# Pairing a gate chunk with a value chunk in one TensorE pass, with a new division of PSUM, in an attention and gated-MLP kernel

## The chip, the cores and the metric

The kernel runs on one core of one Trainium2 chip. The metric is the device time of one execution in microseconds (us), as the median of several executions. "PE" is TensorE (matmuls), "PEld" its weight loads, "DVE" VectorE, "ACT" ScalarE, "POOL" GpSimd.

## The reference, cut to what matters

```python
# x: (4, 12416, 128)   inducing: (32, 128)   4 x 12416 = 49664 tokens
def mab(q, kv):                       # softmax attention, no projections
    s = scale * (q @ kv.transpose(0, 2, 1))
    a = np.exp(s - s.max(-1, keepdims=True))
    a /= a.sum(-1, keepdims=True) + 1e-09
    return a @ kv
h = mab(inducing, x)                  # 32 rows for each batch
y = mab(x, h)                         # 12416 rows for each batch
# ... y as (49664, 128); d_ff = 1536
g   = y @ w_gate
val = y @ w_val
ffn = (gelu(g) * val) @ w_out
out = y + sigmoid(y @ w_res) * ffn
```

Each row of y is a mix of only 32 rows of h. So the kernel never forms y before the first layer: it multiplies h by the first-layer weights once for each batch, and the first layer of a token is then a matmul of its 32 attention weights (kept in four repeated row blocks of 32) with that small matrix.

## The kernel before

Tokens are taken in groups of 512: 24 for each of the four batches, numbered 0 to 23, and a small one of 128 tokens (24). A large group has six slots of two gate and two value chunks. The kernel divides eight PSUM banks of 128 x 512 f32: three buffers of two banks that gates and values share, and two single "side" banks.

```python
    ps_gv = ctx.enter_context(tc.tile_pool(name="psgv", bufs=3, space=bass.MemoryType.PSUM))
    ps_2 = [ctx.enter_context(tc.tile_pool(name=f"ps{i}", bufs=1, space=bass.MemoryType.PSUM))
            for i in range(2)]
    # ... cut
    def slot_mms(gi, si, weights):
        # ... cut: c0, cn, tw, half, rt
        v = wide_bank()
        for c in [i // 2 + (i % 2) * half for i in range(2 * half)]:
            if c < cn:
                r = slice(64, 128) if c >= half else slice(0, 64)
                pe.matmul(v[:, c * tw:(c + 1) * tw],
                          weights[b][r, (c0 + c) * P:(c0 + c + 1) * P], rt[r, :],
                          start=True, stop=True)
        return v[:, :cn * tw]

    def gate_slot(gi, si):
        v = slot_mms(gi, si, hg_t)
        # ... cut
        act.activation(ge[:, :n], v, AC.Gelu, bias=0.0, scale=1.0)        # 1024 wide

    def value_slot(gi, si):
        v = slot_mms(gi, si, hv_t)
        # ... cut
        ve.tensor_tensor(u[:, :n], ge_t.pop((gi, si)), v, AL.mult)        # 1024 wide
```

Two matmuls that use different halves of the array's 128 rows run at the same time (in the trace of this kernel, shown in the prediction, two of 512 columns take 0.39 us together, the line at 781.35). Before, two gate chunks share a pass, then two value chunks. At the end of a group two "mixes" of h (one for the sigmoid's argument, one for y) are made, each of four 128-column matmuls into a side bank, two slots and one slot before the group's last work (arguments shortened with ...):

```python
        def gate(self):
            bank = self.mix(hr_t[self.b])
            self.th = p_fin.tile([P, TOK], FP32, name="th", tag="th")     # p_fin: 2 buffers
            act.activation(self.th[:, :self.tw], bank[:, :self.tw], AC.Tanh, bias=0.0, scale=0.5)

        def residual(self):
            bank = self.mix(ha_t[self.b])
            self.at = p_fin.tile([P, TOK], FP32, name="at", tag="at")     # p_fin: 2 buffers
            act.activation(self.at[:, :self.tw], bank[:, :self.tw], AC.Copy, bias=0.0, scale=1.0)

        def end(self):
            ve.scalar_tensor_tensor(self.th..., self.ffn..., AL.add, AL.mult)     # (tanh + 1) * ffn
            po.tensor_tensor(self.at..., self.at..., self.th..., AL.add)
            sy.dma_start(out[...], self.at...)
    # ... cut: where each piece stands in the order of slots (f: the group's first slot)
            for i in range(6):
                at(f + 2 + i, lambda lg=lg: lg.mms(8))    # output matmuls
            at(f + 5, lg.gate, START)
            at(f + 6, lg.residual, START)
            at(f + 7, lg.end, LATE)
```

While one batch is worked on, the next one is prepared in the background: its scores and exponentials in two "bursts" (with slots that have values only, fed by gates stored ahead), five partial sums in between, and the sums of the second softmax (four reductions on VectorE).

The softmax here doesn't subtract the row's maximum and nothing guards it: scores larger than these inputs give would overflow.

Of the kernel before, what the change touches and what calls it, by code (L numbers as in the profile page):

```python
# [18 lines left out]
def kernel(  # L19
# [51 lines left out]
    p_ge = ctx.enter_context(tc.tile_pool(name="gelu", bufs=6))  # L71
    p_u = ctx.enter_context(tc.tile_pool(name="up", bufs=7))
    p_fin = ctx.enter_context(tc.tile_pool(name="fin", bufs=2))
    ps_gv = ctx.enter_context(tc.tile_pool(name="psgv", bufs=3, space=bass.MemoryType.PSUM))
    ps_2 = [ctx.enter_context(tc.tile_pool(name=f"ps{i}", bufs=1, space=bass.MemoryType.PSUM))
            for i in range(2)]

    ctx.enter_context(tc.manual_schedule())



    parity = [0]

    def side_bank(group):
        return ps_2[group % 2].tile([P, TOK], FP32, name="sb", tag="sb")

    def misc_bank():
        return side_bank(parity[0] + 1)

    def wide_bank():  # L90
        return ps_gv.tile([P, 2 * TOK], FP32, name="gv", tag="gv")
# [40 lines left out]
    def turn_pe(b, k):  # L132
        _, w = blocks_of(k)
        xt = sized(p_xt, w, P, "xt")
        xt_t[b, k] = xt
        tps = wide_bank().bitcast(FP16).rearrange("p (k c) -> p k c", c=P)
        for j in range(w):
            pe.transpose(tps[:, j, :], hi_t[b, k][:, j, :], identF)  # L138
        act.activation(xt[:, :w, :], tps[:, :w, :], AC.Copy, bias=0.0, scale=1.0)  # L139


    nacc_t, acc_t, ha_t, hr_t, hg_t, hv_t, ht_t, hf_t = {}, {}, {}, {}, {}, {}, {}, {}
    e_of = {}

    def scores(b, j0, j1, rows, bank):
        for j in range(j0, j1):
            k, jj = divmod(j, PRE)
            pe.matmul(bank[:, (j - j0) * M:(j - j0 + 1) * M], xt_t[b, k][:, jj, :], rows,  # L148
                      start=True, stop=True)

    def exp_a(b, j0, j1, bank=None):
        n = (j1 - j0) * M
        bank = wide_bank() if bank is None else bank
        scores(b, j0, j1, I1T, bank)
        if n > 2 * M:
            e1 = p_sm.tile([P, 2 * TOK], FP16, name="e1", tag="e1", bufs=3)
        else:
            e1 = p_sm.tile([P, 2 * M], FP16, name="e1s", tag="e1s", bufs=1)
        act.activation(e1[:, :n], bank[:, :n], AC.Exp, bias=0.0, scale=scale)
        for j in range(j0, j1):  # L160
            e_of["a", b, j] = e1[:, (j - j0) * M:(j - j0 + 1) * M]

    def accumulate(b, j0, j1, first, last):
        if first:
            acc_t[b] = misc_bank()
        acc = acc_t[b]
        for j in range(j0, j1):
# [3 lines left out]
            e = e_of.pop(("a", b, j))  # L171
            pe.matmul(o[:, 0:P], e, hi_t[b, k][:, jj, :],  # L172
                      start=(first and j < j0 + Q), stop=False, skip_group_check=True)
            pe.matmul(o[:, P:2 * P + 1], e, lo_t[b, k][:, jj, :P + 1],  # L174
                      start=False, stop=(last and j + Q >= j1), skip_group_check=True)
        if last:
            if b not in nacc_t:
                nacc_t[b] = p_h.tile([P, 2 * P + 1], FP32, name="nacc", tag="nacc", bufs=1)
                ve.tensor_copy(nacc_t[b], acc[:, :2 * P + 1])
            else:  # L180
                na = nacc_t[b]
                ve.tensor_tensor(na, acc[:, :2 * P + 1], na, AL.add)
            del acc_t[b]

    def finish_h(b):
        hs = misc_bank()
        na = nacc_t.pop(b)
        sm = strips.rearrange("p q m -> p (q m)")
        pe.matmul(hs[:, P:P + 1], sm, na[:, 2 * P:2 * P + 1], start=True, stop=True)
        pe.matmul(hs[:, 0:P], sm, na[:, 0:P], start=True, stop=False)  # L190
        pe.matmul(hs[:, 0:P], sm, na[:, P:2 * P], start=False, stop=True)
# [5 lines left out]
        ha = p_h.tile([P, P], FP16, name="ha", tag="ha")  # L197
        ha_t[b] = ha
        po.tensor_copy(ha, hf)
        po.tensor_tensor(ha[M:2 * M, :], hf[M:2 * M, :], ha[M:2 * M, :], AL.subtract)  # L200
        hg_t[b] = p_h.tile([P, F], BF16, name="hg", tag="hg")
        hv_t[b] = p_h.tile([P, F], BF16, name="hv", tag="hv")

    def turn_h(b):
        tp = misc_bank()
# [5 lines left out]
    def first_layer(b, parts, engs):  # L211

        bank = wide_bank()
        o = 0
        for (dst, w, c0, c1), eng in zip(parts, engs):
            o0 = o
            for c in range(c0, c1, TOK):
                e = min(c + TOK, c1)
                pe.matmul(bank[:, o:o + e - c], ht_t[b], w[:, c:e], start=True, stop=True)
                o += e - c  # L220
            if eng is act:
                act.activation(dst[:, c0:c1], bank[:, o0:o], AC.Copy, bias=0.0, scale=0.5)
            else:
                ve.tensor_scalar(dst[:, c0:c1], bank[:, o0:o], 0.5, None, op0=AL.mult)

    hgt_t = {}

    def first_layer_t(b):

        bank = wide_bank()  # L230
        for o, w in ((0, wG), (TOK, wV)):
            for c in range(FCH):
                pe.matmul(bank[:, o + c * M:o + (c + 1) * M], w[:, c * P:(c + 1) * P],
                          ht_t[b][:, 0:M], start=True, stop=True)
        hgt_t[b] = p_h.tile([P, 2, FCH * M], BF16, name="hgt", tag="hgt", bufs=1)
        act.activation(hgt_t[b], bank.rearrange("p (s n) -> p s n", s=2)[:, :, :FCH * M],
                       AC.Copy, bias=0.0, scale=0.5)

    def spread(b, i):

        n = 2 * FCH // 3
        src = hgt_t[b].rearrange("p s (c m) -> p (s c) m", m=M)[:, i * n:(i + 1) * n, :]
        a2 = p_sm.tile([P, PRE, Q, M], BF16, name="a2", tag="a2")
        po.tensor_copy(a2, src.unsqueeze(2).to_broadcast([P, n, Q, M]))
        for dst, c0, c1 in ((hg_t[b], 0, FCH), (hv_t[b], FCH, 2 * FCH)):
            lo, hi = max(c0, i * n), min(c1, (i + 1) * n)
            if lo < hi:
                sy.dma_start_transpose(
                    dst.rearrange("p (c f) -> p c f", f=P)[:, lo - c0:hi - c0, :],
                    a2[:, lo - i * n:hi - i * n].rearrange("p c q m -> p (c q m)"))  # L250

    def res_layer(b):
        bank = misc_bank()
        pe.matmul(bank[:, :P], ht_t[b], wR, start=True, stop=True)
        hr = p_h.tile([P, P], FP16, name="hr", tag="hr")
        hr_t[b] = hr
        act.activation(hr, bank[:, :P], AC.Copy, bias=0.0, scale=1.0)
        ve.tensor_tensor(hr[M:2 * M, :], bank[M:2 * M, :P], hr[M:2 * M, :], AL.subtract)

    def exp_b(b, j0, j1, bank=None):  # L260
        n = (j1 - j0) * M
        bank = wide_bank() if bank is None else bank
        scores(b, j0, j1, ht_t[b][:, 0:M], bank)
        if n > 2 * M:
            e2 = p_sm.tile([P, 2 * TOK], FP32, name="e2", tag="e2", bufs=3)
        else:
            e2 = p_sm.tile([P, 2 * M], FP32, name="e2s", tag="e2s", bufs=1)
        act.activation(e2[:, :n], bank[:, :n], AC.Exp, bias=0.0, scale=scale)  # L268
# [375 lines left out]
```

## Time and profile before

| | before |
|---|---|
| median (4 runs) | 857.7 us (856.9 to 859.5) |
| span of the profiled execution | 855.8 us |
| pace of a group, last batch | 7.76 us |
| group 12 and 13 (first burst) | 10.67 and 8.60 us |
| group 20 and 21 (second burst) | 8.86 and 12.8 us |
| first th | 56.06 us from the start |

The pace and the groups are read from the starts of one instruction, VectorE's (tanh + 1) * ffn, named th in the profile: it comes once in a group, so the distance of two starts is the length of a group. The 100 starts divide the whole span into 101 pieces. In a line of the timeline the columns are start, length, engine, source line, operation, output<-inputs, shapes, and count, then in brackets how long the engine stood idle before it and on whose work. The lengths of several instructions in one line are from the first start to the last end.

### The profile page before, as it was taken

How to read it: one execution, taken by the hardware profiler on the slowest of the kernel's cores; microseconds unless marked ns; L12 is line 12 of the kernel's file. 1: busy time of each engine (PE TensorE's matmuls, PEld its weight loads, DVE VectorE, ACT ScalarE, POOL GpSimd, SP SyncE). 2: the span in 40 equal slices, each digit the busy share in tenths (PEclk: the TensorE clock that was granted, in tenths of full speed). 3: DMA queues.
4: the chain of work that ended last, by engine and by line, in shares of the span. 5: the costliest groups of instructions: out<-in, count | busy, mean ns of one | idle time of the engine just before them, and what ended most of it. 6: DMA issues, size and time to landing. Idle time of an engine off the chain costs nothing.

```text
span 855.8 us, 23356 instructions
## 1 busy us (share of the span) xinstructions
PE 795.1 (93%) x9602; PEld 479.1 (56%) x9602; DVE 796.7 (93%) x784; ACT 734.1 (86%) x861; POOL 356.9 (42%) x313
## 2 busy tenths in 40 slices
PE   5889999999899999999989999999989999999997
PEld 4545556555555555555555555555555555555554
DVE  8699999899999999899999999989999999999997
ACT  5599998888889989888989998988888999988994
POOL 2538885111468766112247867311245611111111
PEclk9599999999999999999999999999999999999999
DMA  8337874010447765101245876200135501010111
GB/s 308 110 85 157 207 176 121 27 38 27 84 96 165 182 172 127 40 26 38 51 88 106 221 163 161 74 31 27 38 64 100 116 26 39 38 39 27 38 38 41
DMA packets 123787, 79.42 MB, mean 93 GB/s; under 512 B 102016, under 2 KB 104736, under 8 KB 123680
## 3 DMA queue, kind: packets, MB, share of 16 engines
q1 hardware_dynamic: 121392, 75.50, 35.4%
q10 hardware_dynamic: 2288, 2.43, 1.0%
q8 instruction: 75, 1.23, 0.7%
q14 instruction: 32, 0.26, 0.1%
HBM read 27.87 MB, written 25.43 MB: 62 GB/s over the span
## 4 chain that ended last, share of the span: by engine, by line
PE 52%; DVE 25%; issue 11%; ACT 8%; DMA 1%; POOL 1%; DVEq 0%; ACTq 0%; POOLq 0%; SPq 0%
PE gv L322 26%; DVE u L338 19%; PE sb L361 19%; ACT ge L331 6%; PE sb L370 5%; DVE lo L123 2%; DVE th L389 1%; DVE z L275 1%; DVE hi L121 1%; PE sb L172 1%; ACT at L384 1%; ACT th L378 1%; DMA ge<-in_moe_w_out_dram 1%; PE sb L174 0%; POOL wO L450 0%
## 5 line engine op out<-in xcount | busy, mean ns | idle before, releaser
L338 DVE TENSOR_TENSOR u<-ge,gv 128x1024 bf16<-128x1024 f32 x584 | 691.1, 1213 | 41.8 <-PE gv L322 26.0
L331 ACT ACTIVATE ge<-gv 128x1024 f32<-128x1024 f32 x584 | 591.7, 1023 | 79.3 <-PE gv L322 67.0
L361 PE MATMUL sb<-wO,u 128*128 128x128 bf16 x4656 | 360.5, 220 | 0.1
L361 PEld LDWEIGHTS <-u 128*128 128x128 bf16 x4656 | 262.1, 98 | 121.4 <-issue 98.9
L392 POOL TENSOR_TENSOR at<-at,th 128x512 f32<-128x512 f32 (+1 forms) x100 | 123.8, 1238 | 407.6 <-ACT ge L331 369.4
L322 PE MATMUL gv<-rt,hv 64*128 64x512 f16 x1152 | 222.5, 378 | 25.6 <-ACT ge L331 9.7
L322 PE MATMUL gv<-rt,hg 64*128 64x512 f16 x1152 | 224.9, 385 | 11.7 <-DVE u L338 6.9
L322 PEld LDWEIGHTS <-hv 64*128 64x128 bf16 x1200 | 99.5, 94 | 103.0 <-issue 88.6
L322 PEld LDWEIGHTS <-hg 64*128 64x128 bf16 x1200 | 63.9, 93 | 76.6 <-issue 16.8
L289 POOL TENSOR_TENSOR a<-e,z 128x1024 f16<-128x1024 f32 (+2 forms) x50 | 91.2, 1832 | 20.8 <-ACT e2s L268 12.9
L370 PEld LDWEIGHTS <-rt 64*128 64x128 f16 x768 | 56.7, 93 | 37.9 <-issue 17.6
L123 POOL TENSOR_TENSOR lo<-xf,hi 128x1024 f16<-128x1024 f32 x36 | 76.8, 2134 | 0.3
L389 DVE SCALAR_TENSOR_TENSOR th<-th,sb 128x512 f32<-128x512 f32 (+1 forms) x100 | 66.4, 664 | 1.8 <-PE sb L361 1.8
L378 ACT ACTIVATE th<-sb 128x512 f32<-128x512 f32 (+1 forms) x100 | 57.9, 579 | 8.8 <-PE sb L370 8.6
L384 ACT ACTIVATE at<-sb 128x512 f32<-128x512 f32 (+1 forms) x100 | 58.0, 580 | 0.8 <-PE sb L370 0.8
L121 POOL CAST hi<-xf 128x1024 f16<-128x1024 f32 x36 | 37.3, 1037 | 22.6 <-DMA xf<-in_x_dram 19.1
L370 PE MATMUL sb<-ha,rt 64*128 64x128 f16 x384 | 36.5, 214 | 0.2
L370 PE MATMUL sb<-hr,rt 64*128 64x128 f16 x384 | 36.6, 215 | 0.0
L148 PEld LDWEIGHTS <-xt 128*128 128x128 f16 x768 | 23.8, 98 | 3.3 <-issue 2.3
L139 ACT ACTIVATE xt<-gv 128x1024 f16<-128x1024 f16 x12 | 12.3, 1024 | 13.4 <-PE gv L138 13.3
L138 PE MATMUL gv<-identF,hi 128*128 128x128 f16 x96 | 11.2, 288 | 9.0 <-DVE hi L121 8.9
L268 ACT ACTIVATE e<-gv 128x1024 f32<-128x1024 f32 (+2 forms) x13 | 11.9, 959 | 7.8 <-PE gv L148 7.8
(93 smaller groups left out, 259.0 us busy)
## 6 DMA issues: line engine op xcount, KB each, us to landing
out_dram<-at SPq DMA_DIRECT2D x96, 256.0 KB, 2.1
xf<-in_x_dram SPq DMA_DIRECT2D x42, 512.0 KB, 4.2
ge<-in_x_dram SPq DMA_DIRECT2D x6, 512.0 KB, 5.8
rt<-a SPq DMA_TRANSPOSE x49, 3.1
xt<-hi SPq DMA_TRANSPOSE x36, 3.3
ge<-in_moe_w_gate_dram ACTq DMA_DIRECT2D x1, 512.0 KB, 4.8
ge<-in_moe_w_val_dram ACTq DMA_DIRECT2D x1, 512.0 KB, 4.3
ge<-in_moe_w_out_dram ACTq DMA_DIRECT2D x1, 512.0 KB, 4.4
```

The costliest lines, as they stand in the source:

```text
L121: e_hi.tensor_copy(hi[:, :w, :], xf[:, :w, :])
L123: e_lo.tensor_tensor(lo[:, :w, :P], xf[:, :w, :], hi[:, :w, :], AL.subtract)
L289: po.tensor_tensor(a2[:, :n], ev[:, o:o + n, :].unsqueeze(2).to_broadcast([P, n, Q, M]), z[:, 1, o:o + n].unsqueeze(2).unsqueeze(3).to_bro ...
L322: pe.matmul(v[:, c * tw:(c + 1) * tw], weights[b][r, (c0 + c) * P:(c0 + c + 1) * P], rt[r, :], start=True, stop=True)
L331: act.activation(ge[:, :n], v, AC.Gelu, bias=0.0, scale=1.0)
L338: ve.tensor_tensor(u[:, :n], ge_t.pop((gi, si)), v, AL.mult)
L361: pe.matmul(self.ffn[:, k, :], u_t[self.gi, si][:, o:o + P], wO[:, fc, :], start=first, stop=not self.todo, skip_group_check=True)
L370: pe.matmul(bank[:, k * P:(k + 1) * P], rt_t[self.b, self.k][r, self.j0 + k, :], h[r, :], start=True, stop=True)
L378: act.activation(self.th[:, :self.tw], bank[:, :self.tw], AC.Tanh, bias=0.0, scale=0.5)
L384: act.activation(self.at[:, :self.tw], bank[:, :self.tw], AC.Copy, bias=0.0, scale=1.0)
L389: ve.scalar_tensor_tensor(self.th[:, :tw], self.th[:, :tw], 1.0, self.ffn.rearrange("p k c -> p (k c)")[:, :tw], AL.add, AL.mult)
L392: po.tensor_tensor(self.at[:, :tw], self.at[:, :tw], self.th[:, :tw], AL.add)
```

## The change

The intent: a gate chunk takes rows 0 to 63 of the array and a value chunk rows 64 to 127, so that one pass makes both; gates get three banks of their own, values two pairs, and one bank is left for the output. With that, the first layer's matrix is packed (gate part in the upper half, value part in the lower), both mixes run in the two row halves in one go, gelu becomes 512 wide, and the row sums of the second softmax move from VectorE to GpSimd. At the start the exponentials become wider and the weights are cast without scaling. The store of gates ahead of values grows from four slots to ten halves.

```diff
-    p_ge = ctx.enter_context(tc.tile_pool(name="gelu", bufs=6))
-    p_u = ctx.enter_context(tc.tile_pool(name="up", bufs=7))
+    p_ge = ctx.enter_context(tc.tile_pool(name="gelu", bufs=7))
+    p_u = ctx.enter_context(tc.tile_pool(name="up", bufs=6))
     p_fin = ctx.enter_context(tc.tile_pool(name="fin", bufs=2))
-    ps_gv = ctx.enter_context(tc.tile_pool(name="psgv", bufs=3, space=bass.MemoryType.PSUM))
-    ps_2 = [ctx.enter_context(tc.tile_pool(name=f"ps{i}", bufs=1, space=bass.MemoryType.PSUM))
-            for i in range(2)]
+    ps_g = ctx.enter_context(tc.tile_pool(name="psg", bufs=3, space=bass.MemoryType.PSUM))
+    ps_v = ctx.enter_context(tc.tile_pool(name="psv", bufs=2, space=bass.MemoryType.PSUM))
+    ps_f = ctx.enter_context(tc.tile_pool(name="psf", bufs=1, space=bass.MemoryType.PSUM))
 # ... cut: sums on Pool, by halving
+            po.tensor_tensor(t[:, :w], ev[:, :, :M // 2], ev[:, :, M // 2:], AL.add)
+            m = M // 4
+            while m > 1:
+                po.tensor_tensor(t[:, :w, :m], t[:, :w, :m], t[:, :w, m:2 * m], AL.add)
+                m //= 2
 # ... cut: slot_mms, gate_slot and value_slot go, and in their place
+    def emit(gate, value):
+        todo = []
+        if gate is not None:
+            gb = bank_g()
+            todo.append(products(*gate, slice(0, 64), gb))
+        if value is not None:
+            i, h = value
+            if h == 0:
+                v_t[i] = bank_v()
+            todo.append(products(i, h, slice(64, 128), v_t[i][:, h * TOK:(h + 1) * TOK]))
+        for n in range(max(map(len, todo))):
+            for t in todo:
+                if n < len(t):
+                    pe.matmul(*t[n], start=True, stop=True)
 # ... cut: gelu of 512 after each gate, product of 1024 after the second value
-        def gate(self):
-            bank = self.mix(hr_t[self.b])
-        def residual(self):
-            bank = self.mix(ha_t[self.b])
+        def mix(self):
+            banks = bank_g(), bank_g()
+            n = self.tw
+            for k in range(self.nk):
+                for r, bank in zip((slice(0, 64), slice(64, 128)), banks):
+                    pe.matmul(bank[:, k * P:(k + 1) * P],
+                              rt_t[self.b, self.k][r, self.j0 + k, :], hra_t[self.b][r, :],
+                              start=True, stop=True)
+            act.activation(self.th[:, :n], banks[0][:, :n], AC.Tanh, bias=0.0, scale=0.5)
+            act.activation(self.at[:, :n], banks[1][:, :n], AC.Copy, bias=0.0, scale=1.0)
 # ... cut: th and at tiles come from p_fin as before
+        at(f + 2, lg.mix, START)
-            for i in range(6):
-                at(f + 2 + i, lambda lg=lg: lg.mms(8))
-            at(f + 5, lg.gate, START)
-            at(f + 6, lg.residual, START)
+            for i, n in enumerate((10, 10, 10, 9, 9)):
+                at(f + 3 + i, lambda lg=lg, n=n: lg.mms(n))
             at(f + 7, lg.end, LATE)
 # ... cut
-    LEAD = 4
+    LEAD = 10
```

## The prediction

> **What bounds the kernel now.** I read first the page's busy shares and the chain that ended last.
>
> ```profile
> PE 795.1 (93%) x9602; PEld 479.1 (56%) x9602; DVE 796.7 (93%) x784; ACT 734.1 (86%) x861; POOL 356.9 (42%) x313
> ...
> PE 52%; DVE 25%; issue 11%; ACT 8%; DMA 1%; POOL 1%; DVEq 0%; ACTq 0%; POOLq 0%; SPq 0%
> ...
> L338 DVE TENSOR_TENSOR u<-ge,gv 128x1024 bf16<-128x1024 f32 x584 | 691.1, 1213 | 41.8 <-PE gv L322 26.0
> L331 ACT ACTIVATE ge<-gv 128x1024 f32<-128x1024 f32 x584 | 591.7, 1023 | 79.3 <-PE gv L322 67.0
> ```
>
> Three engines are above 85% and the chain changes between TensorE and VectorE: no single engine is the bound. The work is 96 groups of 512 tokens (and 4 small ones) of six slots each. A slot is two gate and two value matmuls of 512 columns, one gelu of 1024, one product of 1024, and output matmuls. Spacing the th instruction (one for each group, L389) in the timeline gives the pace: 7.76 us a group, almost to 10 ns, through the undisturbed last 180 us. So I read the timeline of one such group.
>
> ```profile
> 781.35 0.39 PE L322 MATMUL gv<-rt,hg 64*128 64x512 f16 x2
> 781.42 5.84 DVE L338 TENSOR_TENSOR u<-ge,gv 128x1024 bf16<-128x1024 f32 x5
> 781.58 0.38 PE L322 MATMUL gv<-rt,hv 64*128 64x512 f16 x2
> ...
> 781.89 0.62 PE L361 MATMUL sb<-wO,u 128*128 128x128 bf16 x8
> 782.69 0.39 PE L322 MATMUL gv<-rt,hg 64*128 64x512 f16 x2 [0.18 <-DVE u L338]
> ...
> 784.24 0.39 PE L322 MATMUL gv<-rt,hv 64*128 64x512 f16 x2
> 784.45 0.38 PE L370 MATMUL sb<-hr,rt 64*128 64x128 f16 x4
> 784.77 0.62 PE L361 MATMUL sb<-wO,u 128*128 128x128 bf16 x8
> ...
> 786.72 0.39 PE L322 MATMUL gv<-rt,hg 64*128 64x512 f16 x2
> 786.95 0.38 PE L322 MATMUL gv<-rt,hv 64*128 64x512 f16 x2
> 787.16 2.12 ACT L331 ACTIVATE ge<-gv 128x1024 f32<-128x1024 f32 x2
> 787.26 0.62 PE L361 MATMUL sb<-wO,u 128*128 128x128 bf16 x8
> 787.44 1.22 DVE L338 TENSOR_TENSOR u<-ge,gv 128x1024 bf16<-128x1024 f32 x1 [0.18 <-PE gv L322]
> 787.81 0.39 PE L322 MATMUL gv<-rt,hg 64*128 64x512 f16 x2
> 788.23 0.39 PE L322 MATMUL gv<-rt,hv 64*128 64x512 f16 x2
> ```
>
> Distances between starts give prices. Two 512-column matmuls in different row halves already run together: a pair every 0.22 to 0.23 us, gates with gates, values with values. From the last pair to the output matmuls is 0.31; eight of those and the way back is 0.55; one more costs 0.058 ((0.62-0.215)/7). An unstalled slot is 1.09 (786.72 to 787.81). The two slots that carry the mixes (L370, four 128-column matmuls) take 1.50 and 1.40. The wait at 788.23 is the three shared wide buffers: that value pair waits for the gelu of the gates before it (1.51 after its gates). The limiting loop is visible: a product ends, gates go at 782.69, three slots to the values at 786.95, a product at 787.44, th, and again. VectorE alone would need less: products at 1.13 (2.34 us for two, less one of 1.22) and 0.60 for th, 6 x 1.13 + 0.60 = 7.4 us.
>
> **What the Trainium skill says.** "TensorE: Matmul & The Clock Gate", section "Back-to-back issue gap", gives N/2.4 + 2.5 ns for matmuls in a row: 216 ns at 512 columns, 56 at 128; the trace agrees (0.22, 0.058). "TensorEngine Tiling (Array Packing)", "Key Properties", says that changing the tiling mode drains the array and different tiles run in parallel; the trace shows the drain as 0.31 in place of 0.22. Its "Gotcha 1: PSUM Pressure" says different row tiles write different PSUM banks, which the new gate and value banks keep. "Perfetto Trace Analysis", "Tensor Engine Instruction (MATMUL, LD_WEIGHTS)", says TensorE's queue pulls only weight loads ahead: a matmul that waits holds all behind it. The wait at 788.23, with the output matmuls behind it, agrees.
>
> **The change part by part.** *Pairing gate with value* saves no streaming: two pairs of 0.22 a slot before and after. It separates the buffers, so a value no longer waits for a gelu of the same slot; the 0.2 us waits of that kind go. But gates now have banks of 512, so gelu becomes 1168 instructions. ScalarE starts 512 after 512 at 0.48 (at L384 at 786.67, gelu at 787.16) and 1024 after 1024 at 0.92 (exponentials at the start, three in 2.67). Per group 14 x 0.48 = 6.7 us against 6 x 0.92 + 2 x 0.48 = 6.5: more, still under the pace.
>
> *The mix.* Both mixes go together, in row halves, straight after the third slot's pairs: 8 matmuls in about 0.22 and no mode switch for them. That takes some 0.5 us of TensorE from a group. But they take two of the three gate banks at once. With latencies of this trace (gate start to gelu start 0.44, gelu of 512 0.59, its end to TensorE 0.06), t=0 at the first pair of the mix slot, banks A, B, then C and A: the mix into A waits for the first gelu, 0.43+0.59+0.06 = 1.08. Its last C matmul starts at 1.25, ends at 1.46, tanh runs 1.51 to 2.10. The next slot's second gate wants C: 2.16. Then 0.31 to the output matmuls and 0.67 for ten of them: 3.14 us for two slots whose unstalled work is 1.9. The other four slots, with 10, 10, 9, 9 output matmuls, are 2 x 1.21 + 2 x 1.15 = 4.71. TensorE's loop is then **7.85 us a group**. VectorE's products start well within it. So I expect the gain to turn into this wait: 96 x 0.08 = +8 us.
>
> *Batch preparation* now costs 15 us in each of three places (batch period 204.69 against 24 x 7.76 + 3.0). VectorE loses the row sums (1.2 us x 3) and half of each partial sum (0.42 to about 0.28): about 5 us of its work, behind TensorE in my loop. The bursts are one value-only slot with one or two 512-wide exponentials, fed by five slots of stored gates; the two table loads (1.28 each) and the 97 score matmuls (0.03 each, 2.9 us) stay. I count 2.3 us of added TensorE time and 1.7 of restart through three banks, 4 for each of two bursts, where before has 2.9 and 5.0. Each of five partial sums adds the 0.69 of its matmuls less the wait it fills, 0.5, as before. Rebuilding the lead costs eight extra half-gates of 0.22 for each burst. Altogether about 16 against 15: +2 us over three batches.
>
> *Start.* The output weight becomes a plain cast (4.23 us for two scaled ones before, plain 1024 ones 1.04) on GpSimd, ahead of the first weights; the first exponential and sum are four times as wide. I read -1 us. Packed first layer is inside this. Sums on Pool are 10 us a batch on an engine 42% busy.
>
> Sum: 857.6 + 8 + 2 - 1 = about 867.
>
> **Rivals.** *VectorE becomes the bound.* If the gate-bank waits don't close a loop, TensorE has only about 6.6 us of work a group and VectorE saturates. Products spaced 1.155 as in the run of five above make 7.5 us: 96 x 0.26 = -25, and 5 us of VectorE work less in three batches, so about 820. For it speak the lower TensorE work and two value pairs; against it the three banks with four takers in the mix slot.
>
> *The mix doesn't overlap*, or ScalarE becomes a queue: if its eight matmuls come at 0.058 each, tanh and all after it move 0.17 later; 8.0 us a group, about 885. Page support for overlapping halves is good, so less likely.
>
> *GpSimd late:* the reciprocal waits in VectorE's order for the Pool sums. Four slots are 5 us, the sum about 3: hidden, else a few us a batch.
>
> **Range and chances.** I give my loop about 0.6, the saturated VectorE 0.28, the slower mix 0.12. The weighted mean of 867, 820 and 885 is near 856; the median is nearer my loop: 860, range 822 to 885. Faster needs under 840: 0.29. Slower needs over 875: 0.18.
>
> **What would show it.** Right: th spaced 7.8 to 7.9 in the last batch, TensorE idle before the mix and before the next slot's second gate with ScalarE as releaser, VectorE idle about 0.4 us a group. Wrong: th at 7.4 to 7.5 and VectorE without gaps (the first rival), tanh starting later than 1.6 us after its slot's first gate (the second). Burst groups over 4 us above the pace would show my burst count too small.

## The result, and the profile after

The changed kernel took 882.95 us (median of four, 878.94 to 885.81), the kernel before 857.69 in the same rounds. The ratio is 1.0288 (95% interval 1.0244 to 1.0332): slower. A ratio here is the mean time of one kernel's runs over the mean of the other's in the same rounds, so it is not quite the ratio of the two medians. All outputs are right.

First the page of the changed kernel: its busy shares, the chain that ended last, and the groups that answer to those of before.

```profile
PE 787.8 (89%) x9586; PEld 447.7 (51%) x9586; DVE 794.0 (90%) x773; ACT 782.3 (89%) x1462; POOL 380.6 (43%) x376
...
PE 56%; ACT 23%; DVE 13%; issue 4%; DMA 2%; POOL 1%; ACTq 0%; POOLq 0%; SPq 0%; DVEq 0%
...
L350 DVE TENSOR_TENSOR u<-ge,v 128x1024 bf16<-128x1024 f32 x584 | 702.0, 1215 | 71.6 <-PE v L336 33.6
L342 ACT ACTIVATE ge<-g 128x512 f32<-128x512 f32 x1164 | 622.2, 601 | 51.6 <-PE v L336 20.6
...
L384 PE MATMUL g<-hra,rt 64*128 64x128 f16 x768 | 57.6, 218 | 36.1 <-ACT ge L342 31.4
```

TensorE has 7 us less work, VectorE 3 us less, ScalarE 48 us more. Yet TensorE is idle for 96 us (883.8 less 787.8) in place of 61, and VectorE for 90 in place of 59. ScalarE's share of the chain rises from 8% to 23%, and the new mix (L384) alone has 36.1 us of idle ahead of it, 31.4 of them on a gelu. The timeline of one group in the last batch, where nothing is prepared in the background, shows how that comes about (some lines left out).

```profile
800.39 0.39 PE L336 MATMUL g<-rt,hgv 64*128 64x512 f16 x1
...
800.62 0.38 PE L336 MATMUL g<-rt,hgv 64*128 64x512 f16 x1
...
800.83 0.22 PE L384 MATMUL g<-hra,rt 64*128 64x128 f16 x1
801.11 0.68 DVE L394 SCALAR_TENSOR_TENSOR th<-th,f 128x512 f32<-128x512 f32 x1
801.46 0.38 PE L384 MATMUL g<-hra,rt 64*128 64x128 f16 x7 [0.41 <-ACT ge L342]
...
801.71 7.33 DVE L350 TENSOR_TENSOR u<-ge,v 128x1024 bf16<-128x1024 f32 x6
801.90 0.60 ACT L388 ACTIVATE th<-g 128x512 f32<-128x512 f32 x1
801.95 0.37 PE L336 MATMUL g<-rt,hgv 64*128 64x512 f16 x1
...
802.55 0.37 PE L336 MATMUL g<-rt,hgv 64*128 64x512 f16 x1 [0.21 <-ACT th L388]
...
802.88 0.73 PE L373 MATMUL f<-wO,u 128*128 128x128 bf16 x10
```

The two gate chunks take two of the three gate banks at 800.39 and 800.62. The first mix takes the third at 800.83; the second mix has to wait for the first gelu to free a bank, 0.41 us. The next slot's second gate then waits 0.21 for the tanh. After that come the output matmuls. Next group's th starts at 808.96: 7.85 us, where before it was 7.76. VectorE's six products stand in one line of 7.33, but they are not back to back: their starts lie 1.14 to 1.34 apart, where in the run of five shown in the prediction most are 1.13 apart. The records of successive products overlap, so the table by windows below counts only 0.13 us of idle time in this group (7.72 busy of 7.85).

So the steady pace is 0.09 slower, about 8.6 us over the 96 groups. The loss is 25 by the medians, and 28 between the two profiled executions. Splitting their spans at the starts of th shows where the rest lies. The last two columns are experiments told below.

| stretch, us | before | changed | changed + third buffer + early table | split mix + both |
|---|---|---|---|---|
| start to the first th | 56.1 | 58.3 | 56.4 | 56.4 |
| groups 0 to 7, 31 of them | 245.3 | 256.5 | 250.4 | 239.9 |
| groups 8 to 11, batches 0 to 2 | 93.5 | 98.5 | 94.2 | 89.9 |
| groups 12 and 13, three times | 57.8 | 63.1 | 63.6 | 60.0 |
| groups 14 to 19, three times | 153.8 | 156.8 | 156.4 | 149.7 |
| groups 20 to 22, three times | 87.5 | 88.9 | 87.3 | 83.4 |
| groups 23 and 24, three times | 32.6 | 32.0 | 32.1 | 30.3 |
| last batch, 8 to 22 | 116.4 | 117.7 | 117.7 | 112.3 |
| last two groups and the end | 12.9 | 12.1 | 12.1 | 12.2 |
| span | 855.8 | 883.8 | 870.1 | 834.0 |

Two of the large differences are single groups. Group 8 of batch 0 has 12.21 us, and group 0 of batch 3 has 12.43, in place of 7.85 and 8.2. The timeline of the first of them:

```profile
116.96 0.73 PE L373 MATMUL f<-wO,u 128*128 128x128 bf16 x10
...
118.49 0.60 ACT L390 ACTIVATE at<-g 128x512 f32<-128x512 f32 x1 [1.91 <-DMA out_dram<-at]
...
119.14 0.58 PE L336 MATMUL g<-rt,hgv 64*128 64x512 f16 x1 [1.45 <-ACT at L390]
...
120.17 1.25 PE L373 MATMUL f<-wO,u 128*128 128x128 bf16 x10
```

The copy of the second mix (L390) waits 1.91 us for a transfer: its tile is one of only two, and the output two groups earlier still leaves from it. That copy holds a gate bank, so TensorE stands for 1.45 us. And then the ten output matmuls take 1.25 in place of 0.73, and the gates 0.58 in place of 0.37. The table by windows tells why; its columns are window, length, busy time (and count) of PE, PEld, DVE, ACT and POOL, granted TensorE clock, busy share of the DMA engines, GB/s. The first line is that group, the second a group of the first burst, the third an undisturbed one.

```profile
115.19:127.40 12.21, 10.03 (x80) 5.30 (x80) 7.83 (x9) 7.50 (x15) 11.47 (x10) 0.72 0.90 202
...
371.33:382.93 11.60, 10.10 (x125) 5.38 (x124) 8.20 (x9) 9.57 (x19) 1.26 (x1) 0.85 0.07 24
...
801.11:808.96 7.85, 7.12 (x80) 3.85 (x80) 7.72 (x8) 7.49 (x15) 1.27 (x1) 1.00 0.10 35
```

The clock was 0.72 of full in the first, 0.85 in the second: in both, a short idle of TensorE is followed by some microseconds at half rate. In the second it happens with hardly any transfer (DMA share 0.07): group 13 had 11.55, 11.60 and 11.31 us in the three batches, each at 0.85. The second burst shows it too, in two batches of three. Here is group 21 of batch 0, and then of batch 1:

```profile
236.16:245.73 9.57, 8.89 (x82) 4.77 (x81) 7.81 (x8) 7.77 (x16) 7.20 (x11) 0.82 0.08 29
447.08:455.14 8.06, 7.38 (x82) 4.01 (x81) 7.79 (x9) 7.76 (x16) 6.68 (x9) 1.00 0.09 34
```

The third place is the start, first in the kernel before and then in the changed one:

```profile
43.38 1.28 ACT L331 ACT_TABLE_LOAD   x1
...
44.72 0.60 PE L322 MATMUL gv<-rt,hg 64*128 64x512 f16 x4 [0.47 <-DMA rt<-a]
```

```profile
42.81 0.37 PE L336 MATMUL g<-rt,hgv 64*128 64x512 f16 x1
43.26 1.28 ACT L342 ACT_TABLE_LOAD   x1 [1.96 <-issue]
...
45.20 0.37 PE L336 MATMUL g<-rt,hgv 64*128 64x512 f16 x1 [1.58 <-ACT ge L342]
...
50.37 1.25 PE L373 MATMUL f<-wO,u 128*128 128x128 bf16 x10
```

The first gates came 1.9 us earlier than before (44.72 there). But the gelu table is loaded only once the first gate matmul is done, though ScalarE had been idle for 1.96 us. In the trace of the changed kernel a semaphore wait of the gelu's line (L342) stands on ScalarE ahead of the load, from 40.56 to 43.23; in the kernel before the load follows the last exponential at once, and the wait of the gelu's line comes behind it. All three gate banks are full by then, TensorE stops for 1.58 us, and again the output matmuls at 50.37 run at half rate.

### The profile page after: what moved, and what is told of

Read it like the earlier page. It is cut to its first block, busy times and chain, and to the rows that moved or that the text cites. A ratio compares the mean times of both kernels' runs of the same rounds, so it can differ in the third digit from the quotient of the medians.

```text
span 883.8 us, 23924 instructions
## 1 busy us (share of the span) xinstructions
PE 787.8 (89%) x9586; PEld 447.7 (51%) x9586; DVE 794.0 (90%) x773; ACT 782.3 (89%) x1462; POOL 380.6 (43%) x376
## 4 chain that ended last, share of the span: by engine, by line
PE 56%; ACT 23%; DVE 13%; issue 4%; DMA 2%; POOL 1%; ACTq 0%; POOLq 0%; SPq 0%; DVEq 0%
PE f L373 25%; PE g L336 22%; ACT ge L342 17%; DVE u L350 10%; ACT th L388 4%; PE v L336 3%; PE g L157 2%; DVE lo L121 2%; ACT at L390 1%; DMA out_dram<-at 1%; DVE hi L119 1%; PE g L175 1%; POOL at L397 1%; PE g L177 1%; ACT L342 0%
## 5 line engine op out<-in xcount | busy, mean ns | idle before, releaser
L350 DVE TENSOR_TENSOR u<-ge,v 128x1024 bf16<-128x1024 f32 x584 | 702.0, 1215 | 71.6 <-PE v L336 33.6
L342 ACT ACTIVATE ge<-g 128x512 f32<-128x512 f32 x1164 | 622.2, 601 | 51.6 <-PE v L336 20.6
L336 PE MATMUL g<-rt,hgv 64*128 64x512 f16 x1152 | 363.1, 386 | 35.9 <-ACT th L388 15.0
L336 PE MATMUL v<-rt,hgv 64*128 64x512 f16 x1152 | 378.6, 389 | 0.4 <-DVE u L350 0.4
L373 PE MATMUL f<-wO,u 128*128 128x128 bf16 x4656 | 350.8, 223 | 1.0 <-DVE th L394 1.0
L336 PEld LDWEIGHTS <-hgv 64*128 64x128 bf16 x2400 | 102.1, 94 | 151.9 <-issue 83.5
L283 POOL TENSOR_TENSOR a<-eb,z 128x1024 f16<-128x1024 f32 (+1 forms) x49 | 90.9, 1862 | 7.3 <-DMA rt<-a 5.5
L384 PE MATMUL g<-hra,rt 64*128 64x128 f16 x768 | 57.6, 218 | 36.1 <-ACT ge L342 31.4
L384 PEld LDWEIGHTS <-rt 64*128 64x128 f16 x768 | 37.3, 94 | 73.9 <-issue 62.7
L394 DVE SCALAR_TENSOR_TENSOR th<-th,f 128x512 f32<-128x512 f32 (+1 forms) x100 | 66.4, 664 | 1.0 <-PE f L373 1.0
L388 ACT ACTIVATE th<-g 128x512 f32<-128x512 f32 (+1 forms) x100 | 58.5, 585 | 5.8 <-PE g L384 5.5
L390 ACT ACTIVATE at<-g 128x512 f32<-128x512 f32 (+1 forms) x100 | 58.1, 581 | 6.1 <-DMA out_dram<-at 5.0
L119 POOL CAST hi<-xf 128x1024 f16<-128x1024 f32 x36 | 37.3, 1037 | 30.3 <-DMA xf<-in_x_dram 26.1
L157 PEld LDWEIGHTS <-xt 128*128 128x128 f16 x768 | 23.3, 98 | 12.1 <-issue 11.7
L136 PE MATMUL g<-identF,hi 128*128 128x128 f16 x96 | 10.7, 278 | 10.1 <-DVE hi L119 9.9
```

The costliest lines, as they stand in the source:

```text
L119: e_hi.tensor_copy(hi[:, :w, :], xf[:, :w, :])
L283: po.tensor_tensor(a2[:, :n], ev[:, o:o + n, :].unsqueeze(2).to_broadcast([P, n, Q, M]), z[:, o:o + n].unsqueeze(2).unsqueeze(3).to_broadc ...
L336: pe.matmul(*t[n], start=True, stop=True)
L342: act.activation(ge_t[i][:, h * TOK:h * TOK + n], gb[:, :n], AC.Gelu, bias=0.0, scale=1.0)
L350: ve.tensor_tensor(u[:, :n], ge_t.pop(i)[:, :n], v_t.pop(i)[:, :n], AL.mult)
L373: pe.matmul(self.ffn[:, k, :], u_t[self.gi, si][:, o:o + P], wO[:, fc, :], start=first, stop=not self.todo, skip_group_check=True)
```

## The experiments

Twelve kernels ran, in four sets. The runs of one set share a chip and the runs of the kernel before (median 858.0 in the first set, 858.8 in the second, 858.4 in the third, 860.1 in the fourth); "ratio" is always to these. The theory was the prediction's loop of three gate banks. Its first rival was that ScalarE, 89% busy and with 14 instructions a group, had become the queue that everything waits for; the second, that VectorE was the limit already.

### The two mixes apart, one gate bank at a time

```diff
-        def mix(self):
-            banks = bank_g(), bank_g()
+        def mixed(self, r):
+            bank = bank_g()
             for k in range(self.nk):
-                for r, bank in zip((slice(0, 64), slice(64, 128)), banks):
-                    pe.matmul(...)
+                pe.matmul(bank[:, k * P:(k + 1) * P], rt_t[...][r, self.j0 + k, :], hra_t[self.b][r, :], ...)
-        at(f + 2, lg.mix, START)
+        at(f + 2, lg.gate, START)          # rows 0 to 63, tanh
+            at(f + 5, lg.residual, START)  # rows 64 to 127, copy
```

> One part undone: the two mixes no longer go together in row halves; the tanh mix stays behind the third slot's pairs, the attention mix goes behind the sixth slot's. Each takes one gate bank. Theory (the paired mix waits on two of three gate banks, a TensorE-ScalarE loop): though TensorE gets 0.2 us more work a group, the last batch's pace falls from 7.85 us to VectorE's 7.4 to 7.55, and the time by about 96 x 0.35 = 34 us to near 850; since the attention copy comes three slots later its wait for the output DMA goes too (two groups of 12.2 and 12.4 us), so perhaps 840. Rival A (ScalarE is simply too busy with 1168 gelus of 512): pace stays at 7.8 or more, as ScalarE's work is the same. Rival B (the pairing saved TensorE time that is needed): pace rises to 8.0 or more.

The edit does two things: each mix takes one bank at a time, and the second mix stands three slots later. Measured: 843.99 us (841.53 to 847.11), ratio 0.9837 (0.981 to 0.9863), pace 7.49. The timeline of one group, then its line in the table by windows:

```profile
800.52 0.38 PE L381 MATMUL g<-hra,rt 64*128 64x128 f16 x4
...
800.80 0.68 DVE L398 SCALAR_TENSOR_TENSOR th<-th,f 128x512 f32<-128x512 f32 x1
...
801.40 6.98 DVE L350 TENSOR_TENSOR u<-ge,v 128x1024 bf16<-128x1024 f32 x6
...
804.30 0.38 PE L381 MATMUL g<-hra,rt 64*128 64x128 f16 x4
...
808.29 0.68 DVE L398 SCALAR_TENSOR_TENSOR th<-th,f 128x512 f32<-128x512 f32 x1
```

```profile
800.80:808.29 7.49, 7.15 (x82) 4.22 (x80) 7.49 (x8) 7.27 (x15) 1.28 (x1) 1.00 0.10 37
```

VectorE is busy for 7.49 of 7.49 us: six products in 6.98, then th, without a gap. TensorE issues the same matmuls and even pays for two passes of mixes in place of one. So the banks were the limit, and without that wait VectorE nearly is (of the 7.49 us some 0.1 are products that start later than 1.13 after the one before; one wait of 0.25 for a gelu is left ahead of a gate). All of ScalarE's instructions are still there, so ScalarE was not. One group of this run (batch 0, group 11) had 14.81 us:

```profile
140.94 0.60 ACT L388 ACTIVATE th<-g 128x512 f32<-128x512 f32 x1 [5.59 <-POOL at L401]
```

The tanh waited for GpSimd's add, which frees the th tile; the add stood behind the conversions of the next batch. The two buffers for th and at are the limit here too, by another engine.

### A third buffer for th and at

```diff
-    p_fin = ctx.enter_context(tc.tile_pool(name="fin", bufs=2))
+    p_fin = ctx.enter_context(tc.tile_pool(name="fin", bufs=3))
```

> Three buffers in place of two for the tanh and attention tiles at the end; nothing else. Theory: the attention copy on ScalarE in two groups waits 1.8 to 1.9 us for the output DMA of two groups earlier, holds a gate bank, and TensorE idles and then runs at half clock for some 6 us; so with a third buffer the groups of 12.21 us (group 8 of batch 0) and 12.43 us (group 0 of batch 3) become 7.9 to 8.7, the last batch stays at 7.85, and the time falls by 6 to 10 us to about 874. Rival: those two groups are slow for the weights that GpSimd makes late, or for the clock alone; then they stay and the time stays at 882.

Measured: 875.12 us (874.44 to 878.3), ratio 1.0205 (1.018 to 1.0229), 8 us less than the changed kernel. The pace stays at 7.85. Group 8 of batch 0 goes from 12.21 to 7.85 and group 0 of batch 3 from 12.43 to 8.24, and no wait of the copy for a transfer is left in the waits. So the third buffer takes the accident away. Group 13 still has 11.55 to 11.87 us at a clock of 0.85, so that is another cause.

### One more instruction on ScalarE in each group

```diff
+            at(f + 5, lambda: act.activation(spare[:, 1, :], spare[:, 0, :], AC.Copy, bias=0.0, scale=1.0), END)
```

> A cost added: one more ScalarE copy of 128x256 from SBUF to SBUF in each full group, behind the sixth slot's gelus, with no reader. It takes about 0.26 us of ScalarE a group. Theory (loop through the mix slot and the slot after it; elsewhere ScalarE has slack): pace in the last batch stays within 0.03 of 7.85 and the time rises by under 8 us (ramp groups may take some). Rival A (ScalarE's occupancy is the bound): pace rises by 0.26 to 8.1, and the time by about 25 us.

Measured: 883.3 us (881.93 to 885.04), ratio 1.0294 (1.0278 to 1.0309), the same as the changed kernel within the interval. The line of busy shares of its page:

```profile
PE 787.4 (89%) x9585; PEld 448.6 (51%) x9586; DVE 793.9 (90%) x774; ACT 800.6 (91%) x1558; POOL 379.7 (43%) x376
```

ScalarE does 18 us more, and the pace stays at 7.85. An engine in 23% of the chain of waits is not thereby the bound: what counts is when its gelu frees a bank, not how much it does. In two of the three batches of this run group 13 was at full clock, with 10.30 and 10.32 us; the other had 11.38 at 0.85. So half rate costs 1.1 to 1.3 us there, and whether it comes differs from run to run.

### The mix later in its slots

```diff
-        at(f + 2, lg.mix, START)
+            at(f + 3, lg.mix, END)         # behind the slot's output matmuls
```

> The paired mix is kept, with its row halves and both banks, but moved one slot on, behind that slot's ten output matmuls. When it comes up, the first gelu of the slot is done. Theory: the 0.4 us wait of the mix for that gelu goes; the wait of the next slot's second gate for tanh stays (0.2 to 0.6 us); pace 7.4 to 7.6, time about 855 to 862. If the wait were not in the loop, or pairing itself were bad, the pace would stay 7.85.

Measured: 863.97 us (861.86 to 865.72), ratio 1.0066 (1.0044 to 1.0089), pace 7.73. The pace was expected at 7.4 to 7.6 and the time at 855 to 862: right in direction, wrong in size. The waits for a gate bank's tanh, first of the changed kernel, then of this one (us in total, times, longest):

```profile
PE g L336 <- ACT th L388: 15.0, 69, 0.4
```

```profile
PE g L336 <- ACT th L388: 29.3, 89, 0.8
```

The wait of the second mix for the gelu is all but gone (1.2 us in total, 32.6 in the changed kernel), but the wait of the next slot's gate for the tanh has doubled. Two banks taken at once must be given back by two ScalarE instructions in a row, wherever they stand. Only taking one at a time, in the first experiment, removed both.

### The two repairs together

The split mix and the third buffer, as shown above.

> The two mends together: mixes apart (third and sixth slot) and three buffers for the tanh and attention tiles. Theory: pace 7.49 as with the split alone, and the one group of 14.81 us in batch 0 (tanh waited 5.6 us there for GpSimd's late last addition to free its tile) becomes 7.5 to 7.9: about 7 us less than the split alone, 836 to 838, faster than the kernel before by 2.3%. Rival (GpSimd's backlog only moves elsewhere): a group of 10 us or more appears near the same place and the time stays above 841.

Measured: 839.61 us (838.44 to 840.66), ratio 0.978 (0.9761 to 0.9799), pace 7.49, and the group of 14.81 is gone. The time is a little above the 836 to 838 expected. The profiled run had its first th at 60.76, 4.7 us later than the kernel before: the start had to be looked at.

### The old lead of four

```diff
-    LEAD = 10
+    LEAD = 4
```

> As the two mends together, but the stored lead of gates is 4 halves in place of 10. Theory on the ramps: each group of a ramp costs 0.30 us (7.79 against 7.49) for a half-gate that streams with no value beside it, and with six ramp groups less in seven ramps 12 us are saved; but each of six bursts of exponentials then has two slots of gates in store in place of five, so VectorE stands for about three slots more, 3 x 1.2 = 3.6 us each, 22 us. Net 5 to 15 us slower than with 10. Rival (the ramps cost more than the store gives): faster than with 10.

Measured: 841.42 us (838.81 to 843.3), ratio 0.9799 (0.9771 to 0.9828): 2 us slower than with ten by the medians, a difference that the intervals do not separate, and not 5 to 15. The two groups of the first burst are 13.70 and 8.29 in batch 0 (9.53 and 9.90 with ten), and the first long one of the second 14.65 (11.81). But the groups in which the store is filled again become faster, from 7.79 to 7.49 after the second burst and from 8.28 to about 7.96 after the first. In the profiled executions the burst groups cost 15 us more, where the expectation had counted 22, and the other groups give 13 back.

### The sums on GpSimd, alone in the kernel before

```diff
-    p_u = ctx.enter_context(tc.tile_pool(name="up", bufs=7))
+    p_u = ctx.enter_context(tc.tile_pool(name="up", bufs=6))      # room for the partial sums
-            for i in range(4):
-                bg(21, 3 + i, lambda: norm_b(nb, *e2s.pop(0)))
+            for i in range(4):
+                bg(21, 3 + 4 * i, lambda: zs.append(sums_pool(nb, *e2s.pop(0))))
+                bg(21, 7 + 4 * i, lambda: ones_ve(*zs.pop(0)), LATE)
```

> The kernel before with one part of the change alone: the row sums of batches 1 to 3 on GpSimd in halving additions, reciprocals four slots later on VectorE, first weights four slots later (one buffer of the product tile less, for room). Theory: here VectorE and TensorE share the loop, and the second burst group of 12.78 us has 4.9 us of sums and reciprocals on VectorE, of which the sums go: 2 to 3 us less in each of three batches, 849 to 853. Rival (those sums were hidden behind TensorE's burst): the same time, 858.

Measured: 855.45 us (854.53 to 856.5), ratio 0.9968 (0.9945 to 0.999). The group of the burst falls from 12.78 to 10.71, but the two after it rise, from 7.5 and 7.83 to 8.11 each. Of the expected 5 to 9 us some 3 are left. What takes the rest back was not looked into: the edit also makes the first weights four slots later and leaves one buffer less for the products.

### The sums back on VectorE in the changed kernel

```diff
-                at(tb + 4 * n, lambda i=i: sums_b(nb, i, po))
+                at(tb + 4 * n, lambda i=i: sums_b(nb, i, ve))
```

> The changed kernel with that part undone: row sums of batches 1 to 3 back on VectorE, all else as changed. Theory (TensorE's loop through the mix slot sets the pace, VectorE has 0.4 us of slack a group): 3.5 us more of VectorE work a batch over four groups, of which about half is hidden: 0 to 5 us slower than the changed kernel, 882 to 888. Rival (the sums on GpSimd are a cost, as VectorE then waits for GpSimd): 3 or more us faster.

Measured: 888.24 us (887.0 to 890.09), ratio 1.0349 (1.0327 to 1.0371), about 5 us more than the changed kernel. Groups 21 and 22 grow to 9.36 to 10.7 from 8.06 to 9.57. But this run also had waits for a transfer of its own (a group of 10.48 and one of 12.54), half rate in two of the groups 21, and full rate in all three groups 13, so it leaves open how much of the 5 us is the sums; the last set asks again.

### The gelu table ahead of the first gates

On top of the split mix and the third buffer:

```diff
+    act.activation(spare, parts, AC.Gelu, bias=0.0, scale=1.0)     # one column, result not used
     warm = bank_f()
     for i in range(10):
         pe.matmul(warm, wG[:, :P], wG[:, :TOK], start=True, stop=True)
```

> The two mends together, and one gelu of a 128x1 constant right behind the last exponential of the start, so that the gelu table is loaded there. In the changed kernel and in all the experiments the first table load comes 0.44 us after the first gate matmul in place of ahead of it, since the first gelu's wait for that gate was put on the load. Theory: the load (1.28 us) leaves the path; TensorE then doesn't idle 1.58 us there, and doesn't run at half clock afterwards (about 3 us lost in the profiles). First th at 55 to 57 us against 60.8 (or 57.4 in the split alone), 2 to 5 us less than the 839.6 of the two mends. Rival (the half clock comes from something else): only 1.3 us less.

Measured: 834.72 us (833.33 to 836.1), ratio 0.9716 (0.9697 to 0.9735), the fastest kernel of all here. Its start:

```profile
41.24 1.28 ACT L495 ACT_TABLE_LOAD   x1
...
44.45 0.39 PE L336 MATMUL g<-rt,hgv 64*128 64x512 f16 x1
...
45.57 0.37 PE L336 MATMUL g<-rt,hgv 64*128 64x512 f16 x1 [0.30 <-ACT ge L342]
...
49.81 0.73 PE L373 MATMUL f<-wO,u 128*128 128x128 bf16 x10
```

The load is done before the gates come, TensorE stands for 0.30 in place of 1.58 us, the ten output matmuls take 0.73, and the first th is at 56.35 in place of 60.76. Not all of these 4.4 us are the load's: the first gates came at 44.45 in place of 45.99, ahead of anything that the load delays. From the first gate to the first th it is 11.90 in place of 14.77.

### A lead of six in that kernel

```diff
-    LEAD = 10
+    LEAD = 6
```

> As with the early table load, and a stored lead of 6 half-gates in place of 10. From the two runs with 10 and 4: four ramp groups less of 0.30 us each in seven ramps (8 us less), against two slots less of store in six bursts (a burst pair cost 22.0 to 22.6 against 19.4 to 19.8 us in the first and 22.4 against 19.5 to 21.0 in the second, for three slots less; so about 4 us for two slots in each pair of bursts, 12 us in three batches). Expected within 5 us of the same kernel with 10, more likely slower.

Measured: 838.17 us (836.28 to 839.44), ratio 0.9758 (0.9741 to 0.9775), 3.5 us slower, as the expectation leaned. Ten is kept.

### The sums back on VectorE in that kernel

The same edit as above, on the fastest kernel.

> The kernel of the early table load (ratio 0.9716 to before) with its row sums back on VectorE, four wide reductions of about 1.2 us in each of three batches. There the moved work is tested without the output DMA's accident and without the late start, which the run with sums on VectorE in the changed kernel had. Theory (VectorE is the bound of this version, so 3.6 us a batch of sums come back nearly whole, 10.8 us in all, less where it was idle): 840 to 845 us, ratio 0.978 to 0.984, the two groups after the second burst longer by 2.5 to 3.5 us together. Rival (what the other run lost was its accidents and not the sums): within 2 us of 834.7, ratio below 0.974.

Measured: 843.54 us (841.84 to 844.59), ratio 0.9806 (0.9791 to 0.9821). As expected. By the ratios the sums on GpSimd are worth 0.0090 of 858, about 8 us, where VectorE is the bound. In its timeline a reduction stands between the products as before:

```profile
431.09 1.21 DVE L255 TENSOR_REDUCE z<-eb 128x32 f32<-128x1024 f32 x1
```

Groups 21 and 22 are 9.64 and 9.36 us (one group 21 10.33), with GpSimd 7.72 and 8.29.

### The changed kernel with the third buffer and the early table, the mix left paired

> The changed kernel with three final buffers and the gelu table loaded ahead of the first gates, its mix left paired. It closes the account of the loss: 875.1 us of the three buffers less some 3 to 4 us of the start is 870 to 873 us, ratio 1.015 to 1.019; first th at 55.5 to 57 us; the steady pace stays 7.85 and the ramp groups 8.17. If the start is not worth what the early table load gave in the other version (4.9 us), it stays at 874 to 876. The groups after the first burst may be 11.5 at a clock of 0.85 or 10.3 at the full clock, which shifts it by up to 4 us.

Measured: 872.04 us (870.24 to 873.54), ratio 1.0137 (1.0119 to 1.0155). The time and the first th (56.40) are as expected, the ratio just below its range, as the kernel before was slower on this chip. The pace is 7.85, and group 13 is at 0.85 of the clock in all three batches (11.55, 11.59 and 11.87). This closes the account: from here to the fastest kernel only the split of the mix is left, and it takes the ratio from 1.0137 to 0.9716, 36 us of 858. The difference of pace, 0.36 over 96 groups, is 34.6 of them by calculation; half rate also differs between the two profiled executions (group 13 at 0.85 in three batches here, in one there), so the two numbers agree only to some us.

## Why the prediction was right or wrong

**The loop: right.** The prediction said 7.85 us a group, TensorE idle before the mix and before the next slot's second gate with ScalarE as releaser. The trace has 7.85, with waits of 0.41 and 0.21 in those two places, and the steps between agree too: counted from the first pair of the mix's slot, the second mix was foreseen at 1.08, tanh at 1.51 and the next slot's second gate at 2.16, and the trace has them at 1.07, 1.51 and 2.16. That is not luck. The split mix shows that this wait is the cause: with it gone the pace is 7.49. The sign "VectorE idle about 0.4 us a group" holds for the spacing of the products (7.85 less the 7.4 that the prediction gives VectorE alone), not for the idle time that the profile counts, 0.13. One citation of the prediction is loose: the section "Back-to-back issue gap" of the Trainium skill calls the formula the gap of isolated matmuls, and gives about 81 ns for 128 columns in a stream with weight loads. The trace, a stream with weight loads, has 58 ns, so the prices that were used stand.

**VectorE's pace as the rival: its number right, its condition not met.** The rival put a saturated VectorE at 7.5 us a group, 25 us, and 5 us of VectorE work less in each of three batches besides, together about 820. VectorE does run at 7.49 once the mix is split. But the whole came to 844, and to 835 with two more repairs, not to 820: the pace brought its 26 us (0.27 over 96 groups), and what the rival counted beyond it does not show in the whole, although the sums alone are worth about 8 us there; where those went was not traced.

**ScalarE as a queue, or mixes that don't overlap: did not come.** That rival had tanh start later than 1.6 us after its slot's first gate; it starts 1.51 after it. ScalarE took 18 us more work with no change of the time beyond the interval.

**The batch preparation: right but for one term.** The prediction counted 16 us for each of three places. Between the th of group 0 in batches 1 and 2 the changed kernel with its accident and its start repaired needs 208.61 us; less 24 x 7.85 and the small group's 3.24 that leaves 17.0. Of this about 1.3 us is half rate of TensorE in the first burst (11.55 and 11.59 against 10.30 at the full clock), which the prediction did not have: 3.6 us in the three batches of the changed kernel's profile, and 3.0 more in its second bursts (9.57 against 8.06, twice). Its own sign of an error, burst groups over 4 us above the pace, is just reached: the first group of the second burst has 11.89, 4.04 above; but the one after it is only 0.2 above at the full clock, so the two together cost the 4 us that were counted.

**The start: wrong in sign.** The step "I read -1 us" fits as far as the first gates go: in the two profiled executions they came 1.9 us earlier, with the ten matmuls before them at the same 2.32 us. Whether the wider exponentials and the plain casts did that was not tested. It did not ask where the gelu table would be loaded. The first th came 2.2 us later, so that term was off by 3. With the early table and the same paired mix it comes at 56.40 in place of 58.28.

**A wait that no step named.** The mixes were moved ahead, from the fifth and sixth slot after the group's first to the second, while the add and the transfer that end a group stayed where they were. So the two tiles of at are asked for sooner, and wherever GpSimd is busy with the next batch, the copy waits for the transfer, holds a gate bank, and TensorE falls to half rate. The prediction does not mention these two buffers; the diff leaves their number unchanged, but not their use. Two such groups, 8 us by the run with three buffers.

**The sum.** The prediction added 8 + 2 - 1 = 9 us. Between the two profiled executions, from which the groups are read, there are 28.0: 8.6 for the loop + 1 for the preparation at full clock (15.7 against 15.4, three times) + 2.2 for the start + 8.6 for the two groups (12.21 and 12.43 less 7.85 and 8.2) + 1.4 for group 0 of batches 1 and 2 (8.65 and 9.19 against 8.24 with three buffers) + 3.6 and 3.0 for half rate in the bursts = about 28. The profiled execution of the changed kernel is the slowest of its four; by the medians the loss is 25. The terms that failed are the last five, and the larger of them are stops of TensorE of 0.8 to 1.6 us with the half rate after them, which the prediction would have had to look for outside the steady group. The measured time lies within the range that was given, but that is luck: the upper end of 885 came from mixes that don't overlap, at 8.0 us a group, and these did not come; terms that nobody had counted filled the same room. The chance of slower by over 2% was put at 0.18. The sum of the main line stood only 8 us from that limit, and the stops that it had not counted could only lengthen it.

**The sums on GpSimd: not late, as predicted.** They were worth about 3 us in the kernel before and 8 where VectorE is the bound; in the changed kernel about 5 was measured, mixed with accidents of that run. VectorE's reciprocal never waits for GpSimd there: its line (L269) is not among the waits.

**What stays open.** What decides whether TensorE falls to half rate was not settled (group 13: at 0.85 in all three batches of some runs, in one or none of others, with the same instructions). The traces show more than the bursts of one kernel. From 60 us on, the eight idles of TensorE of 1.43 us and more in all profiled runs were followed by half rate. Of those of 0.84 to 1.41 us some were and some were not, even for the same instructions: with a lead of six, 1.41 us at 145.8 was followed by a clock of 1.00 over 7 us, and 1.41 at 346.2 by 0.54. In the kernel before, 1.08 us in the second burst was not followed by it in any of the three batches. The spread of the first th, 53.47 to 56.40 among the profiled runs with the early table, is partly explained: the first gate comes at 41.58 to 44.45 in them, since the ten warm-up matmuls before it take 2.3 to 4.2 us. From that gate it is 11.9 in three of the four, and 13.66 in the fourth, where the clock was 0.88. Why the warm-up matmuls differ is open.

## What to carry to other kernels

Count how many buffers one step takes at once, and when each is given back: three banks with a step that takes two at a time cost 0.36 us a group here, and taking them one by one, at the price of more passes, gave 36 us of 858. When a producer is moved earlier, count the buffers between it and the last reader again, even where the diff leaves their number alone. And look at each stop of TensorE twice, for what comes after it: here stops of 0.84 us and more were in part followed by some microseconds of half rate, which can cost more than the stop (group 21 with and without them, 9.57 and 8.06).

## What the Trainium skill lacked or had wrong

- "TensorE: Matmul & The Clock Gate", section "HAM oscillation — how this bites in real kernels", puts the abstract rule as no idle gaps above about 3.4 us. Here an idle of 1.45 us was followed by half rate (ten matmuls in 1.25 us in place of 0.73, mean clock 0.72 over 12.2 us). In the first burst the longest single idle was 0.93 us, and the clock of the group was still 0.85. The page's next section, "A second HAM failure mode: psum-queue depth-cycling", does say that frequent short idles make the clock swing, but gives no length for them. Nor do the runs show a threshold: idles of 0.84 to 1.41 us were followed by half rate in some places and not in others.
- "ScalarE: Activation LUTs", section "What ACT_TABLE_LOAD costs", gives 1283 ns and a drain of 1380 ns for a switch. The load is 1.28 us in every trace here, but no drain of that length shows: in the last experiment the one-column gelu started 0.01 us after the load ended (load at 40.83 for 1.28, gelu at 42.12), and the load 0.02 us after the exponential before it. The page also doesn't say that a load may come only behind the wait of its first activation, so that it isn't hidden in idle time: at the start this took the idle of TensorE from 0.30 to 1.58 us.
- None of the pages consulted gives a price in time for changing the tiling mode; here the step from row halves to the full array took 0.31 us where a pair without it takes 0.22.
